# Retention attention with a SoLU layer behind it: two neighbouring tokens on a partition, fewer and longer loads, some transposes by DMA, and w_out centred once

## The chip, the cores and the metric

The kernel runs on one core of a Trainium2 chip. The core has the engines PE (matmul, with its weight loads), DVE (VectorE), ACT (ScalarE), POOL (GpSimd) and SP, which here only hands out DMA transfers, and sixteen DMA engines. The time is the device time of one execution in microseconds (us), as the median of several runs.

## What is computed

A retention attention without softmax over 8 batches, 8 heads, 576 tokens and a head size of 64, then a layer with SoLU, layer norm and an output projection over the 4608 tokens. Inputs and output are float32.

```python
scores = (q @ k.T) / sqrt(64)
rel = pos[:, None] - pos[None, :]
ret = scores * where(rel >= 0, gamma[h] ** rel, 0)      # gamma[h] = 1 - 2 ** (-5 - h)
x = (ret @ v)                                            # [4608, 512] after joining the heads
h = x @ w_in                                             # [4608, 1024]
e = exp(h - max(h)); solu = h * e / (sum(e) + 1e-9)
ln = (solu - mean(solu)) / sqrt(var(solu) + 1e-6) * g_ln
out = ln @ w_out                                         # [4608, 512]
```

## The kernel before

**Tiles.** Two batches are worked on side by side, one on partitions 0 to 63 and one on 64 to 127. A *pair* is 128 tokens of each of the two batches; 576 tokens make four long pairs and a short one of 64 tokens, and 4 times 2 batches make 20 pairs, four of them short. Each pair gives *chunks* of 128 tokens for the layer behind the attention: two from a long pair, one from a short one, 36 in all, numbered 0 to 35.

**Loads.** `load` (line 165) brings q, k and v of a pair as float32 into a ring of 14 slots in SBUF, one slot a tensor and pair. Each tensor of a long pair takes four transfers: two groups of 64 tokens (`s`) for each of two batches (`x`). A partition holds the tokens p and p + 64, and each piece that is contiguous in DRAM is one head's 64 numbers, 256 bytes.

**Attention.** `cast` (line 191, and 117 or 115 where no table is applied) makes float16 copies, with powers of gamma multiplied into q and v. `turn` (line 215) transposes q and k on PE against an identity, eight 128 x 128 blocks a tensor, into PSUM; `back` copies them to SBUF (`qT`, `kT`). `sc` (line 279) multiplies; a long pair's scores are three blocks of 64 tokens for each head, since the fourth is in the future. `mask` (line 303, steps `m0` and `m1`) multiplies with the 0/1 table `keep`. `kp`, `t`, `s16` and `s32` carry the state on from pair to pair, `xs` applies it, `xv` (line 391) adds the values, `xT` copies a chunk's x, already transposed, to SBUF.

**The layer.** `mm1` (line 483) gives h in two PSUM banks; `max` (line 501), `exp` (526), `solu` (558, with the sum of its result), `nmu` (565), `uc` (572: subtracts the mean), `sq` (579: sum of squares), `w1`, `w2` (586) and `pow` (592) give the factor of the layer norm. `lp` (601) transposes the centred tile on PE, `uT` copies it out, `mm2` (623) multiplies with `w_out16`, which has g_ln in it, and `osb` (643 on ACT, 639 on DVE) scales the rows into one of four output tiles. `st` (line 657; 654 for pair 0 and the short pairs) sends the tile to DRAM.

**Order.** Nothing is scheduled while it runs. The string `PLAN` lists every step with its tile, its engine (`@v` DVE, `@s` ACT, `@g` POOL) and its PSUM banks, and each engine works through its own part in that order. All loads and stores stand in SP's queue, in the plan's order: a transfer that has to wait holds back all that stand behind it. At the start, `warm` puts matmuls on zeros between the first steps.

Of the kernel before, what the change touches and what calls it, by code (L numbers as in the profile page):

```python
# [17 lines left out]
def _np_tables():  # L18


    g = 1.0 - 2.0 ** (-5.0 - np.arange(H, dtype=np.float64))
    i = 64 * np.arange(2)[None, :] + (np.arange(P) % 64)[:, None]
    gq = (g[None, None, :] ** i[:, :, None]) / 8.0
    gk = g[None, None, :] ** (-i[:, :, None])
    gs = np.zeros((P, 4))
    for e in range(2):
        for hp in range(4):
            gs[e * 64 : e * 64 + 64, hp] = g[2 * hp + e] ** 128.0
    return np.concatenate([gq.reshape(P, 16), gk.reshape(P, 16), gs], axis=1).astype(np.float32)
# [3 lines left out]
def kernel(  # L33
# [19 lines left out]
    CROSS = 2  # L53
    SPLIT = (35,)
# [25 lines left out]
    small = sb.tile([P, 36], FP, name="small")  # L80
    gq = small[:, 0:16].rearrange("p (s h) -> p s h", s=2)
    gk = small[:, 16:32].rearrange("p (s h) -> p s h", s=2)
    gs = small[:, 32:36]
    keep = sb.tile([P, 192], FP, name="keep")
    ident = sb.tile([P, P], F16, name="ident")
    zeros = sb.tile([P, 512], F16, name="zeros")
    mhalf = sb.tile([P, 1], FP, name="mhalf")
# [3 lines left out]
    w_x16 = sb.tile([P, 4, DFF], F16, name="w_x16") if CROSS else None  # L91
    w_out16 = sb.tile([P, NF, DM], F16, name="w_out16")
    ring = sb.tile([P, 14, 1024], FP, name="ring")
# [10 lines left out]
    def banks(bs):  # L104
        if len(bs) == 1:
            return pb[:, bs[0] : bs[0] + 1]
        a, b = bs[:2]
        return pb[:, a : b + 1 : b - a]
# [31 lines left out]
    def halves(n, j):  # L140
        if j is not None:
            return [j]
        return [0] if short(n) else [0, 1]

    def span(n, j):
        hs = halves(n, j)
        return slice(hs[0], hs[-1] + 1)


    def slot(name, n):  # L150
        i = "qkv".index(name)
        if n < 2:
            return (0, 7)[n] + i
        return (3 * (n - 2) + i) % 14

    def tok(name, n):
        return ring[:, slot(name, n)].rearrange("p (s h d) -> p s h d", s=2, h=H)

    def load(name, src, n, j):
        g, c = pairs[n]  # L160
        t = tok(name, n)
        for s in halves(n, j):
            for x in range(2):
                r = 64 * (2 * c + s)
                nc.sync.dma_start(  # L165
                    out=t[64 * x : 64 * x + 64, s],
                    in_=src[2 * g + x, :, r : r + 64, :].rearrange("h p d -> p h d"),
                )
# [16 lines left out]
    def cast(name, n, j, eng, table):  # L185
        for s in halves(n, j) if table is not None else [span(n, j)]:
            src, t = tok(name, n)[:, s], t16(name, n)[:, s]
            if table is None:
                copy(eng, t, src)
            else:  # L190
                vec(eng).tensor_tensor(  # L191
                    out=t, in0=src, in1=table[:, s].unsqueeze(2).to_broadcast([P, H, D]),
                    op=ALU.mult,
                )
# [14 lines left out]
    def turn(name, n, j, bs):  # L209
        t = pb[:, bs[0]].bitcast(F16).rearrange("p (s a c) -> p s a c", s=2, a=4)  # L210
        src = t16(name, n)
        for s in halves(n, j):
            s2 = src[:, s].rearrange("p h d -> p (h d)")
            for hp in range(4):
                nc.tensor.transpose(
                    out=t[:, s, hp], in_=s2[:, hp * P : (hp + 1) * P], identity=ident
                )
# [5 lines left out]
    def back(name, n, j, eng):  # L223
        b = T["t" + name, n, j]
        hs = span(n, j)
        w = slice(hs.start * 256, hs.stop * 256)
        t = turned(name, n).rearrange("p s a c -> p (s a c)")
        if eng == "s":
            copy("s", words(t)[:, w], pb[:, b, w])
        else:  # L230
            w2 = slice(w.start * 2, w.stop * 2)
            copy("v", t[:, w2], pb[:, b].bitcast(F16)[:, w2])
# [19 lines left out]

    def blocks(n, j):
        if short(n) or j == 0:
            return 0, 1
        return (1, 3) if j == 1 else (0, 3)

    def per_bank(n, j):
        lo, hi = blocks(n, j)
        return 8 // (hi - lo) if hi - lo < 3 else 2  # L260

    def scores(n, j, bs, e, hp):
        lo, hi = blocks(n, j)
        w = 64 * (hi - lo)
        k = min(per_bank(n, j), 4)
        at = w * (hp % k)
        return pb[:, bs[2 * (hp // k) + e], at : at + w]

    @step
    def sc(n, j, eng, bs):  # L270
        lo, hi = blocks(n, j)
        qt, kt = turned("q", n), turned("k", n)

        def one(e, hp, key, a, b):
            r = slice(64 * e, 64 * e + 64)
            o = scores(n, j, bs, e, hp)[:, 64 * (a - lo) : 64 * (b - lo)]
            for x in range(2):
                c = slice(64 * x, 64 * x + 64)
                nc.tensor.matmul(  # L279
                    out=o[c], lhsT=kt[r, key, hp, c],  # L280
                    rhs=qt[r, a - key : b - key, hp, c], start=True, stop=True,
                )

        rows = []
        for e in range(2):
            rows.append([])
            for hp in range(4):
                a, b = max(lo, 0), min(hi, 2)
                rows[e].append((b - a, lambda e=e, hp=hp, a=a, b=b: one(e, hp, 0, a, b)))
                if hi == 3:  # L290
                    rows[e].append((1, lambda e=e, hp=hp: one(e, hp, 1, 2, 3)))
        together(rows)
        T["sc", n, j] = bs

    def ret(n):
        return buf("ret", n, 2, [P, 2, 4, 192], F16)

    def mask(n, j, i):
        lo, hi = blocks(n, j)
        k = min(per_bank(n, j), 4)  # L300
        bs = T["sc", n, j][2 * i : 2 * i + 2]
        w = 64 * (hi - lo)
        nc.vector.tensor_tensor(  # L303
            out=ret(n)[:, :, k * i : k * i + k, 64 * lo : 64 * hi],
            in0=banks(bs)[:, :, 0 : k * w].rearrange("p e (a c) -> p e a c", a=k),
            in1=keep[:, 64 * lo : 64 * hi].unsqueeze(1).unsqueeze(1).to_broadcast([P, 2, k, w]),
            op=ALU.mult,
        )
# [14 lines left out]
    def xs(n, j, eng, bs):  # L323
        T["x", n, j] = bs
        qt = turned("q", n)
        hs = span(n, j)
        a, b = hs.start * 64, hs.stop * 64
        st = T["s16", n]
        w = b - a

        def one(x, e, hp):
# [3 lines left out]
                out=o[out_half(n, x, e), hp, a:b], lhsT=st[r, x, hp],  # L335
                rhs=qt[r, hs, hp, 64 * x : 64 * x + 64],
# [3 lines left out]
        rows = [[], []]  # L340
        if crossed(n):
            for hp in range(4):
                for e in range(2):
                    rows[e].append((w, lambda e=e, hp=hp: (one(0, e, hp), one(1, e, hp))))
        else:
            for x in range(2):
                for hp in range(4):
                    for e in range(2):
                        rows[e].append((w, lambda x=x, e=e, hp=hp: one(x, e, hp)))
        together(rows)  # L350
# [9 lines left out]
    def kp(n, j, eng, bs):  # L360
        k16, v16 = t16("k", n), t16("v", n)

        def one(x, s, hp):
            r = slice(64 * x, 64 * x + 64)
            o = pb[:, bs[x], 0:256].rearrange("p (a d) -> p a d", a=4)
# [8 lines left out]
            [(64, lambda x=x, s=s, hp=hp: one(x, s, hp)) for hp in range(4) for s in range(2)]  # L374
            for x in range(2)
        ])
        T["kp", n] = bs

    @step
    def xv(n, j, eng, bs):  # L380
        old = ("x", n, j) in T
        bs = T.setdefault(("x", n, j), bs)
        lo, hi = blocks(n, j)
        v16 = t16("v", n)
        rt = ret(n)

        def one(x, key, hp, a, b):
            r = slice(64 * x, 64 * x + 64)
            o = pb[:, bs[x]].rearrange("p (a c) -> p a c", a=4)
            for e in range(2):  # L390
                nc.tensor.matmul(  # L391
                    out=o[out_half(n, x, e), hp, 64 * (a - key) : 64 * (b - key)],
                    lhsT=v16[r, key, 2 * hp + e], rhs=rt[r, e, hp, 64 * a : 64 * b],
                    start=not old and key == 0 and hp == 0, stop=True, skip_group_check=True,
                )

        rows = []
        for x in range(2):
            rows.append([])
            for hp in range(4):  # L400
                a, b = lo, min(hi, 2)
                rows[x].append((b - a, lambda x=x, hp=hp, a=a, b=b: one(x, 0, hp, a, b)))
                if hi == 3:
                    rows[x].append((1, lambda x=x, hp=hp: one(x, 1, hp, 2, 3)))
        together(rows)
# [5 lines left out]
    def t(n, j, eng, bs):  # L411
        g, c = pairs[n]
        kp = banks(T["kp", n])[:, :, 0:256].rearrange("p x (a d) -> p x a d", a=4)
        s = state("ts", n, FP)
        if c == 0:
# [26 lines left out]
    def xT(m, j, eng, bs):  # L442
        n, i = pair_of[m]
        eng = eng or "s"
        if short(n) or n == 0:
            src = banks(T["x", n, i if n == 0 else None]).rearrange("p x (a c) -> p x a c", a=4)
            copy(
                eng, xt(m).rearrange("p a (x c) -> p x a c", x=2),
                src[:, :, :, 64 * i : 64 * i + 64],
            )  # L450
        else:
            b = T["x", n, None][i]
# [43 lines left out]
    def tiny(name, m, j=None, depth=6):  # L496
        return buf(name + sfx(j), m, depth, [P, 1], FP)
# [17 lines left out]
    def u_of(m):  # L515
        return buf("u", m, 2, [P, DFF], F16)

    def uc_of(m):
        return buf("uc", m, 3, [P, DFF], F16)
# [29 lines left out]
    @step  # L549
    def w1(m, j, eng, bs):  # L550
        s = tiny("s", m)
        nc.gpsimd.tensor_scalar(
            out=tiny("w1", m), in0=s, scalar1=s, scalar2=1e-6 * DFF, op0=ALU.mult, op1=ALU.mult
        )
# [23 lines left out]
    def sq(m, j, eng, bs):  # L578
        nc.scalar.activation(  # L579
# [283 lines left out]
```

## Time and profile before

| | |
|---|---|
| Median of three runs | 250.69 us (249.96 to 250.76) |
| The profiled execution | 250.73 us |
| Its span, from the first instruction to the last | 249.0 us |
| Mean granted clock of PE | 0.978 |
| DMA in all | 43.53 MB in 122532 packets, 116096 of them under 512 bytes |
| Landing of a load of 128 KB, median | 3.4 to 3.5 us |

The profile gives for each engine the time in which it was busy, in groups of equal instructions; the waits, with the engine that ended them; stretches of the span with the busy time of each engine; and the chain that ended last, which is followed back from the last instruction to whatever released it at each step. "SPq" is SP's queue at work on handing out transfers, and a line number is that of the kernel. The time from issue to landing of a transfer is taken up to its completion.

### The profile page before, as it was taken

What the parts mean: (1) busy time and instruction counts of PE and PEld (TensorE: products, weight loads), DVE (VectorE), ACT (ScalarE), POOL (GpSimd) and SP (SyncE); (2) the same over time, 40 slices, a digit from 0 to 9 for tenths busy, and PEclk for the clock granted to TensorE, in tenths of its full rate; (3) what the DMA queues carried; (4) which work ended last, traced back from release to release, by engine and by line L of the source; (5) the groups of instructions that cost most, each with busy time, mean ns of one, the idle gap of its engine ahead of it and who ended that gap; (6) DMA issues with size and microseconds to landing.
All of it is one profiled execution on the core that took longest, in us unless ns stands there. A gap on an engine that the chain in (4) does not pass through costs nothing.

```text
span 249.0 us, 7816 instructions
## 1 busy us (share of the span) xinstructions
PE 215.7 (87%) x3175; PEld 120.8 (49%) x3175; DVE 196.3 (79%) x342; ACT 152.9 (61%) x278; POOL 146.0 (59%) x196
## 2 busy tenths in 40 slices
PE   8997878967988887987569999899959999999992
PEld 2543534542553554544326754565527455555642
DVE  0646869993989977688708999997968999999971
ACT  1334747562873677638706858788747667577881
POOL 2054459672777785498356279469398917653330
PEclk9999999997999999999958999999999999999999
DMA  5997898797788788787888887887766446411025
GB/s 114 217 323 165 187 282 191 172 227 158 180 181 244 170 185 201 160 219 209 181 188 203 202 212 196 192 228 205 176 149 202 99 143 155 129 46 42 3 87 170
DMA packets 122532, 43.53 MB, mean 175 GB/s; under 512 B 116096, under 2 KB 116352, under 8 KB 122368
## 3 DMA queue, kind: packets, MB, share of 16 engines
q1 hardware_dynamic: 122352, 43.01, 70.0%
q8 instruction: 25, 0.41, 0.7%
q14 instruction: 11, 0.09, 0.1%
q10 hardware_dynamic: 144, 0.02, 0.1%
HBM read 32.53 MB, written 9.44 MB: 169 GB/s over the span
## 4 chain that ended last, share of the span: by engine, by line
SPq 28%; PE 26%; DVE 16%; DMA 15%; issue 5%; POOL 5%; ACT 3%; DVEq 0%; ACTq 0%; POOLq 0%
SPq L165 23%; PE pb L623 10%; PE pb L483 7%; DMA ring<-in_q_dram 5%; DMA ring<-in_v_dram 4%; DVE u L558 4%; DVE nm L501 3%; DMA ring<-in_k_dram 3%; DMA ring<-in_moe_w_out_dram 3%; DVE ret L303 3%; PE pb L601 3%; POOL v L191 2%; DVE uc L572 2%; SPq L654 2%; PE pb L391 1%
## 5 line engine op out<-in xcount | busy, mean ns | idle before, releaser
L623 PE MATMUL pb<-w_out,uT 128*128 128x512 f16 (+1 forms) x296 | 67.0, 374 | 5.6 <-DVE uT L117 2.5
L526 ACT ACTIVATE e<-pb,nm 128x1024 f32<-128x1024 f32 (+1 forms) x37 | 40.4, 1092 | 17.9 <-DVE nm L501 15.0
L501 DVE TENSOR_REDUCE nm<-pb 128x1 f32<-128x1024 f32 x35 | 42.3, 1217 | 10.2 <-PE pb L483 10.0
L191 POOL TENSOR_TENSOR v<-ring,small 128x512 f16<-128x512 f32 x35 | 36.9, 1072 | 15.1 <-DMA ring<-in_v_dram 15.1
L483 PEld LDWEIGHTS <-xT 128*128 128x128 f16 x280 | 27.0, 100 | 36.6 <-issue 9.1
L623 PEld LDWEIGHTS <-uT 128*128 128x128 f16 x296 | 27.7, 98 | 34.5 <-issue 6.6
L558 DVE SCALAR_TENSOR_TENSOR u<-pb,e 128x1024 f16<-128x1024 f32 (+1 forms) x37 | 43.9, 1187 | 0.6 <-ACT e L526 0.2
L579 ACT ACTIVATE sq<-uc 128x1024 f16<-128x1024 f16 (+1 forms) x37 | 38.4, 1039 | 9.0 <-DVE uc L572 7.1
L483 PE MATMUL pb<-w_in,xT 128*128 128x512 f16 x168 | 39.9, 379 | 1.9 <-DVE w_in L117 1.7
L191 POOL TENSOR_TENSOR q<-ring,small 128x512 f16<-128x512 f32 x30 | 31.5, 1060 | 14.8 <-DMA ring<-in_q_dram 12.3
L303 DVE TENSOR_TENSOR ret<-pb,keep 128x768 f16<-128x768 f32 (+2 forms) x36 | 32.0, 917 | 0.5 <-PE pb L279 0.5
L483 PE MATMUL pb<-w_x,xT 128*128 128x512 f16 x112 | 29.5, 411 | 2.6 <-DMA w_x<-w_in 2.6
L592 POOL TENSOR_TENSOR rs<-w,mhalf 128x1 f32<-128x1 f32 x36 | 20.0, 561 | 19.7 <-DVE w L586 16.0
L572 DVE TENSOR_SCALAR uc<-u,nmu 128x1024 f16<-128x1024 f16 (+1 forms) x37 | 26.5, 719 | 1.0
L643 ACT ACTIVATE osb<-pb,rs 128x512 f32<-128x512 f32 x26 | 17.5, 686 | 15.3 <-POOL rs L592 6.3
L115 ACT CAST xT<-pb 128x512 f16<-128x512 f32 x28 | 15.7, 588 | 13.8 <-PE pb L391 13.8
L601 PE MATMUL pb<-ident,uc 128*128 128x128 f16 x288 | 21.6, 220 | 2.9 <-DVE uc L572 2.9
L115 ACT COPY uT<-pb 128x512 f32<-128x512 f32 x30 | 17.2, 586 | 9.5 <-PE pb L601 9.4
L117 POOL CAST k<-ring 128x1024 f16<-128x1024 f32 (+1 forms) x14 | 13.2, 945 | 16.3 <-DMA ring<-in_k_dram 16.3
L423 POOL TENSOR_TENSOR s<-ts,small 128x512 f16<-128x512 f32 x16 | 17.4, 1089 | 7.2 <-DVE ts L418 5.1
L601 PEld LDWEIGHTS <-uc 128*128 128x128 f16 x288 | 17.1, 98 | 8.9 <-DVE uc L572 5.7
L716 PE MATMUL pb<-zeros 128*128 128x512 f16 x63 | 18.6, 425 | 1.2 <-DVE mhalf L818 1.2
(62 smaller groups left out, 255.5 us busy)
## 6 DMA issues: line engine op xcount, KB each, us to landing
ring<-in_k_dram SPq DMA_DIRECT2D x72, 128.0 KB, 3.4
ring<-in_q_dram SPq DMA_DIRECT2D x72, 128.0 KB, 3.5
ring<-in_v_dram SPq DMA_DIRECT2D x72, 128.0 KB, 3.4
out_dram<-osb SPq DMA_DIRECT2D x30, 256.0 KB, 3.0
ring<-in_moe_w_in_dram SPq DMA_DIRECT2D x4, 512.0 KB, 5.4
ring<-in_moe_w_out_dram SPq DMA_DIRECT2D x4, 512.0 KB, 8.8
out_dram<-osb SPq DMA_DIRECT2D x10, 128.0 KB, 2.8
w_x<-w_in SPq DMA_DIRECT2D x2, 512.0 KB, 4.8
```

Of the source, the lines that this page charges most:

```text
L115: nc.scalar.copy(out=out, in_=in_)
L165: nc.sync.dma_start(out=t[64 * x : 64 * x + 64, s], in_=src[2 * g + x, :, r : r + 64, :].rearrange("h p d -> p h d"),)
L191: vec(eng).tensor_tensor(out=t, in0=src, in1=table[:, s].unsqueeze(2).to_broadcast([P, H, D]), op=ALU.mult,)
L303: nc.vector.tensor_tensor(out=ret(n)[:, :, k * i : k * i + k, 64 * lo : 64 * hi], in0=banks(bs)[:, :, 0 : k * w].rearrange("p e (a c) -> p ...
L483: nc.tensor.matmul(out=pb[:, bs[i]], lhsT=s[:, d], rhs=w[:, d, i * 512 : (i + 1) * 512], start=r == 1, stop=r == 4,)
L501: nc.vector.tensor_reduce(out=tiny("nm", m, j), in_=h_of(m, j), axis=AX.X if j is not None else AX.XY, op=ALU.max, negate=True,)
L526: nc.scalar.activation(out=like_h(e_of(m), j), in_=h_of(m, j), func=ACT.Exp, bias=tiny("nm", m), accum_out=tiny("s", m, j),)
L558: nc.vector.scalar_tensor_tensor(out=like_h(u_of(m), j), in0=h_of(m, j), scalar=1.0, in1=like_h(e_of(m), j), op0=ALU.mult, op1=ALU.mult, a ...
L572: nc.vector.tensor_scalar(out=uc_of(m)[:, cols(j)], in0=u_of(m)[:, cols(j)], scalar1=tiny("nmu", m), scalar2=None, op0=ALU.add, op1=ALU.by ...
L579: nc.scalar.activation(out=buf("sq", 0, 1, [P, DFF], F16)[:, cols(j)], in_=uc_of(m)[:, cols(j)], func=ACT.Square, accum_out=tiny("ss", m, j),)
L601: nc.tensor.transpose(out=t[:, c], in_=u[:, a * P : (a + 1) * P], identity=ident)
L623: nc.tensor.matmul(out=pb[:, bs[0], 0:w], lhsT=ut(m)[:, c], rhs=w_out16[:, c, a : a + w], start=c == 0, stop=c == NF - 1,)
```

## The change

**Two neighbouring tokens on a partition.** Partition p of a long pair now holds the tokens 2p and 2p + 1 instead of p and p + 64, so that each contiguous piece of a load is 128 numbers, and one transfer a tensor and batch is enough: six a pair instead of twelve. The tables of powers follow the new places of the tokens.

```diff
-    i = 64 * np.arange(2)[None, :] + (np.arange(P) % 64)[:, None]
+    p = np.arange(P) % 64
+    i = np.stack([2 * p, 2 * p + 1, p], axis=1)
...
-        for s in halves(n, j):
-            for x in range(2):
-                r = 64 * (2 * c + s)
-                nc.sync.dma_start(
-                    out=t[64 * x : 64 * x + 64, s],
-                    in_=src[2 * g + x, :, r : r + 64, :].rearrange("h p d -> p h d"),
-                )
+        for x in both(j):
+            t = ring[64 * x : 64 * x + 64, slot(name, n)]
...
+                t = t.rearrange("p (h d) -> p h d", h=H)
+                s = src[2 * g + x, :, P * c : P * c + P, :].rearrange("h (p s) d -> p h (s d)", s=2)
+            nc.sync.dma_start(out=t, in_=s)
```

The scores of a long pair are now four blocks of 64 tokens for each head instead of three, because either place of a partition can be before the other one's token; `mask` works on 1024 instead of 768 columns, and `keep` is [128, 5, 64]. The output of a chunk of a long pair has the rows in the order of the places, and the store puts them back in order:

```diff
             r = (2 * g + i) * S + c * P
-            q_.dma_start(out=out[r : r + P, a : a + w], in_=t)
+            q_.dma_start(
+                out=out[r : r + P, a : a + w].rearrange("(p s) m -> s p m", s=2), in_=t
+            )
```

Chunks of pair 0 are stored in this way too; only the short pairs keep the two stores of 64 rows.

**q and k of six pairs transposed by DMA.** For the pairs 7, 8, 10, 12, 13 and 15 the steps `dq` and `dk` take the place of `tq`, `qT`, `tk` and `kT`:

```diff
+    def by_dma(name, n):
+
+        k = 4 * len(places(n))
+        nc.sync.dma_start_transpose(
+            out=turned(name, n).rearrange("p s a c -> p (s a) c")[:, 0:k],
+            in_=t16(name, n).rearrange("p s h d -> p (s h d)")[:, 0 : k * P],
+        )
```

**w_out centred from chunk 8 on.** With `RAW = 8`, chunks from 8 on leave `uc` out: `lp` transposes the tile as it is, `sq` takes the mean as the bias of its square, and `mm2` multiplies with `w_mid16`, a second copy of w_out from which the mean of each column is taken away. The copy is made once, in eight steps `ce` on DVE; `mean` and `evm` give the column means by eight matmuls and a copy.

```diff
     def uc_of(m):
-        return buf("uc", m, 3, [P, DFF], F16)
+        return buf("uc", m, 3, [P, DFF], F16) if m < RAW else u_of(m)
...
     def sq(m, j, eng, bs):
+        by = {} if m < RAW else {"bias": tiny("nmu", m)}
...
+    def ce(c, j, eng, bs):
+        nc.vector.scalar_tensor_tensor(
+            out=w_mid16[:, c], in0=w_out32[:, c], scalar=g32[:, c : c + 1], in1=mean_sb,
+            op0=ALU.mult, op1=ALU.subtract,
+        )
```

w_out in float32 now has a place of its own, and the ring of loads has 10 slots instead of 14. `w1`, `w2` and `pow` are done once for the two chunks of a pair, on [128, 2], but for the first pair and pair 18.

**First pair by halves.** The first pair is loaded, cast, turned, scored and masked by batch, 64 partitions at a time, instead of by groups of 64 tokens; its first `mm1` begins after the first batch. Where before had 63 warming matmuls, there are now 31.

**The plan.** The whole string `PLAN` is written anew, with the new steps in it.

More of the change, by code (lines that the diff above doesn't have):

```diff
@@ L138, in step, with places, rows, both @@
         return f
-    def halves(n, j):
-        if j is not None:
-            return [j]
+    def places(n):
         return [0] if short(n) else [0, 1]
-    def span(n, j):
-        hs = halves(n, j)
-        return slice(hs[0], hs[-1] + 1)
+    def rows(j):
+        return slice(0, P) if j is None else slice(64 * j, 64 * j + 64)
+    def both(j):
+        return [0, 1] if j is None else [j]
     def slot(name, n):
@@ L185, in cast @@
     def cast(name, n, j, eng, table):
[L186 to L194, printed above, removed]
+        r = rows(j)
+        ns = len(places(n))
+        src = ring[r, slot(name, n), 0 : ns * 512].rearrange("p (h s d) -> p s h d", s=ns, h=H)
+        t = t16(name, n)[r, 0:ns]
+        if table is None:
+            copy(eng, t, src)
+            return
+        for s in range(ns):
+            by = table[r, 2 if short(n) else s].unsqueeze(2).to_broadcast([t.shape[0], H, D])
+            vec(eng).tensor_tensor(out=t[:, s], in0=src[:, s], in1=by, op=ALU.mult)
     @step
@@ L248, in kT, with scores @@
         back("k", n, j, eng or "s")
[L253 to L267, printed above, removed]
+    def scores(n, bs, e, hp, s):
+        if short(n):
+            return pb[:, bs[e], 64 * hp : 64 * hp + 64]
+        at = (2 * (hp % 2) + s) * P
+        return pb[:, bs[2 * (hp // 2) + e], at : at + P]
@@ L284, in sc @@
[L284 to L292, printed above, removed]
+                    out=scores(n, bs, e, hp, s)[c], lhsT=kt[r, s, hp, c],
+                    rhs=qt[r, 0:ns, hp, c], start=True, stop=True,
+                )
@@ L293, in sc, with kept @@
+        together([
+            [(1, lambda e=e, hp=hp, s=s: one(e, hp, s)) for hp in range(4) for s in places(n)]
+            for e in range(2)
+        ])
         T["sc", n, j] = bs
     def ret(n):
-        return buf("ret", n, 2, [P, 2, 4, 192], F16)
+        return buf("ret", n, 2, [P, 2, 2, 2, 2 * P], F16)
+    def kept(n, x, e, hp, s):
+        r = slice(64 * x, 64 * x + 64)
+        if short(n):
+            return ret(n)[r, 0, e].rearrange("p a c -> p (a c)")[:, 64 * hp : 64 * hp + 64]
+        return ret(n)[r, hp // 2, e, hp % 2, P * s : P * s + P]
@@ L298, in mask @@
     def mask(n, j, i):
-        lo, hi = blocks(n, j)
-        k = min(per_bank(n, j), 4)
+        r = rows(j)
+        p = r.stop - r.start
         bs = T["sc", n, j][2 * i : 2 * i + 2]
[L302 to L308, printed above, removed]
+        out = ret(n)[r, i].rearrange("p e a c -> p e (a c)")
@@ L373, in kp @@
         together([
[L374 to L375 removed]
+            [(1, lambda x=x, s=s, hp=hp: one(x, s, hp)) for hp in range(4) for s in range(2)]
+            for x in both(j)
         ])
[L377 removed]
+        T["kp", n, j] = bs
     @step
@@ L382, in xv, with one @@
         bs = T.setdefault(("x", n, j), bs)
-        lo, hi = blocks(n, j)
         v16 = t16("v", n)
-        rt = ret(n)
-        def one(x, key, hp, a, b):
+        w = 64 * len(places(n))
+        def one(x, s, hp):
             r = slice(64 * x, 64 * x + 64)
-            o = pb[:, bs[x]].rearrange("p (a c) -> p a c", a=4)
+            o = pb[:, bs[x if j is None else 0]].rearrange("p (a c) -> p a c", a=4)
             for e in range(2):
                 nc.tensor.matmul(
-                    out=o[out_half(n, x, e), hp, 64 * (a - key) : 64 * (b - key)],
-                    lhsT=v16[r, key, 2 * hp + e], rhs=rt[r, e, hp, 64 * a : 64 * b],
-                    start=not old and key == 0 and hp == 0, stop=True, skip_group_check=True,
-                )
[L397 to L405, printed above, removed]
+                    out=o[out_half(n, x, e), hp, 0:w], lhsT=v16[r, s, 2 * hp + e],
+                    rhs=kept(n, x, e, hp, s), start=not old and s == 0 and hp == 0, stop=True,
+                    skip_group_check=True,
+                )
+        together([
+            [(1, lambda x=x, s=s, hp=hp: one(x, s, hp)) for hp in range(4) for s in places(n)]
+            for x in both(j)
+        ])
     def state(name, n, dtype):
```

358 lines of the change are left out of this document (193 added, 165 removed).

## The prediction

> **What bounds the kernel now.** I read the page's shares first, then the chain that ended last, then stretches of time.
>
> ```profile
> span 249.0 us, 7816 instructions
> PE 215.7 (87%) x3175; PEld 120.8 (49%) x3175; DVE 196.3 (79%) x342; ACT 152.9 (61%) x278; POOL 146.0 (59%) x196
> ...
> SPq 28%; PE 26%; DVE 16%; DMA 15%; issue 5%; POOL 5%; ACT 3%; DVEq 0%; ACTq 0%; POOLq 0%
> SPq L165 23%; PE pb L623 10%; PE pb L483 7%; DMA ring<-in_q_dram 5%; DMA ring<-in_v_dram 4%; DVE u L558 4%; DVE nm L501 3%; DMA ring<-in_k_dram 3%; DMA ring<-in_moe_w_out_dram 3%; DVE ret L303 3%; PE pb L601 3%; POOL v L191 2%; DVE uc L572 2%; SPq L654 2%; PE pb L391 1%
> ```
>
> PE is busiest, but the longest entry of the chain is SP's queue handing out the loads of line 165: 23% of 249.0 us, 57 us. The view of that line shows why:
>
> ```profile
> L165 SPq DMA_DIRECT2D ring<-in_k_dram x72: 595/633/3674, 0.8 to 193.6; - x72
> L165 SPq DMA_DIRECT2D ring<-in_q_dram x72: 595/634/2518, 2.3 to 208.8; - x72
> L165 SPq DMA_DIRECT2D ring<-in_v_dram x72: 595/633/1872, 6.3 to 203.8; - x72
> ```
>
> Each of 216 loads holds SP for 0.633 us (median), 137 us together, up to 208.8 us. The stretches (columns: stretch, its length, busy time of PE, weight load, DVE, ACT, POOL, granted clock, DMA share, GB/s) show what the compute engines reach meanwhile:
>
> ```profile
> 65.00:205.00 140.00, 122.60 (x1924) 70.83 (x1925) 117.79 (x204) 92.01 (x167) 93.89 (x119) 0.98 0.76 188
> 144.00:165.00 21.00, 20.14 (x337) 11.58 (x336) 19.94 (x37) 15.55 (x30) 15.86 (x21) 1.00 0.82 199
> ```
>
> Where nothing is late PE is busy 20.14 of 21 us (96%); over the whole middle 122.6 of 140 (88%). So before, the middle is a mixture: PE and DVE near their limit, with late loads in between.
>
> **The stores, which decide.** The 30 whole stores of before are 128 rows of 2 KB:
>
> ```profile
> L657 SPq DMA_DIRECT2D out_dram<-osb x30: 332/432/2144, 76.1 to 243.9; - x30
> DMA to landing us min/median/max: 2.1/3.0/4.5
> ```
>
> After, a partition holds token 2p or 2p+1, so the rows of one 128-partition tile go to DRAM in the order "all even tokens, then all odd ones". In the changed program's list of SP's instructions these 32 stores (256 KB each) have a destination of 2 x 64 rows of 512 numbers, against 128 partitions on the SBUF side. Everything that before moves begins with a count of 64 or 128 on both sides. The trace shows no transfer that begins with 2, so its cost has two ends. If it is still shared by 16 DMA engines, it stays at 3.0 us to landing. If a transfer is shared out by whole steps of its first count, the two sides have only 2 such steps in common, and two engines carry 64 rows (128 KB) each. [...]
>
> [...]
>
> What can an engine carry? Four stretches say it:
>
> ```profile
> 16.00:24.00 8.00, 6.31 (x31) 2.71 (x29) 3.69 (x5) 3.07 (x6) 4.04 (x4) 1.00 0.91 191
> 220.00:244.00 24.00, 23.67 (x250) 13.21 (x235) 20.93 (x50) 19.12 (x39) 8.68 (x17) 1.00 0.15 56
> 13.00:16.00 3.00, 3.00 (x75) 1.58 (x74) 1.31 (x3) 1.24 (x2) 1.14 (x3) 1.00 1.01 385
> 32.00:34.00 2.00, 2.00 (x11) 0.88 (x9) 0.01 (x1) 0.07 (x1) 1.26 (x2) 1.00 1.08 389
> ```
>
> The last two are backlogs, and the share stops at about 1: an engine takes one packet after another, so times add. 16 to 24 us holds loads alone, in rows of 256 bytes: 191/0.91/16 = 13.1 GB/s an engine, 19.5 ns a row. 220 to 244 us holds stores alone: 56/0.15/16 = 23.3 GB/s, 88 ns a row of 2 KB. (The best of any stretch is 385/1.01/16 = 23.8.) The new loads have rows of 512 bytes, which before has not; on the straight line through the two that is 29 ns, 17.5 GB/s. Its ends are 13.1 and 23.3.
>
> **The sum, for one of the two engines.**
> - Stores: 32 x 131,072 bytes at 23.3 GB/s = 5.63 us each, 180 us (176 at 23.8).
> - Loads of the 16 long pairs: 96 of 256 KB, a sixteenth each, 16,384 bytes at 17.5 = 0.94 us: 90 us (68 to 120 at the ends).
> - Loads of the four short pairs: 24 x 8,192 bytes at 13.1: 15 us.
> - Weights and the crossed copy: 10 x 32,768 bytes at 23.3: 14 us.
> - DMA transposes, which before has not: 12 of 256 KB, 16,384 bytes an engine, at 23.3 or, as rows of 256 bytes, at 13.1: 0.70 to 1.25 us each. Between ends so near I take 1.0: 12 us.
> - Short stores, ten, still by 64 rows: 3 us.
>
> Together 314 us for engines that can start at 1 us. That is more than the 249.0 of the whole span, so the two engines set the end; the rest is how well they are kept fed. Before the first such store SP's list has 30 long and 6 short loads and the ten transfers of weights, 28 + 4 + 14 = 46 us of it. In the trace the first store stands at
>
> ```profile
> 65.74 1.22 SPq L654 DMA_DIRECT2D out_dram<-osb  x2
> ```
>
> behind an SP queue full of loads; with 120 loads instead of 216 it comes earlier. I put it at 50 us, so 4 us idle. The other 314 - 46 = 268 us follow, and 2 us for the last landing (2.1 was the least): span 320, and 1.7 more for the execution around it (250.73 against 249.0). An engine that is fed can be a little better than these averages, so I round down to **320 us**. The profiled execution of before (250.73) lies at the upper end of its runs (median 250.69), so no correction is needed.
>
> Does the wait reach the compute engines? The output tile has four buffers, and already before
>
> ```profile
> SPq L657 <- ACT osb L643: 24.6, 6, 8.6
> ACT osb L643 <- DMA out_dram<-osb: 5.8, 2, 3.1
> ```
>
> SP stands 24.6 us before stores whose tile isn't written, and ACT 5.8 us before tiles whose store isn't out. After, the second grows: a chunk costs an engine 5.6 us for its store and 2.8 us for half a pair's loads, 8.4, against (249 - 65.7)/36 = 5.1 us at which before finishes chunks from its first store on. Four tiles on, ACT's scaling of the output (or DVE's) waits for a landing; behind it stand exp, the squares and the PSUM copies, so DVE and PE wait next, and the load queue behind the next store on SP.
>
> **The other edits cost nothing here, because the two engines' 314 us cover them.** What they would be without that cover:
>
> ```profile
> L572 DVE TENSOR_SCALAR uc<-u,nmu 128x1024 f16<-128x1024 f16 x35 | 25.9, 740 | 0.9
> L558 DVE SCALAR_TENSOR_TENSOR u<-pb,e 128x512 f16<-128x512 f32 x2 | 1.4, 691 | 0.2 <-ACT e L526 0.2
> L303 DVE TENSOR_TENSOR ret<-pb,keep 128x768 f16<-128x768 f32 x30 | 27.4, 946 | 0.2 <-PE pb L279 0.2
> L303 DVE TENSOR_TENSOR ret<-pb,keep 128x1024 f16<-128x1024 f32 x1 | 1.2, 1224 | 0.3 <-PE pb L279 0.3
> L586 DVE TENSOR_TENSOR w<-w,ss 128x1 f32<-128x1 f32 x36 | 12.2, 344 | 3.6 <-POOL w L552 3.3 <-ACT sq L579 0.3
> L215 PE MATMUL pb<-ident,q 128*128 128x128 f16 x144 | 12.1, 222 | 1.2 <-POOL q L191 0.7 <-DVE q L191 0.5
> L215 PE MATMUL pb<-ident,k 128*128 128x128 f16 x144 | 11.8, 225 | 1.0 <-POOL k L117 0.9
> ```
>
> DVE: 27 centrings gone (-20.0), eight centrings of w_out, priced as the half-width product (+5.5), 30 masks of 1024 instead of 768 (+8.3), 14 of 36 sums gone (-4.8): -11 us. PE: q and k of six pairs are 96 transposes at 23.9/288 = 83 ns (-8.0), while scores and values with 128 columns throughout add about 2.7: -5 us in the middle; 8 matmuls for the column means and 32 fewer warming ones lie near the start. SP: 216 loads become 120 (137 to 76 us), and the 12 transposes stand in the same queue, each behind POOL's cast of q or k, with all later loads and stores queued behind it. First pair by halves: six issues of 0.633 us instead of twelve, up to 4 us earlier. The ring of 10 slots for 14 costs nothing where the engine, not the slot, is late.
>
> **Rivals.**
> - *The stores keep 16 engines: faster.* Then each is 8 rows an engine, 0.70 us, the DMA sum falls to 314 - 180 + 22 = 156 us, and SP no longer sets the pace. Four engines are enough for this: 134 + 90 = 224 us, below the span of before. The middle goes to PE's 96%: (122.6 - 5.3)/0.96 = 122 instead of 140, and 250.7 - 18 = **233 us**. For it: nothing in the trace forbids it. Against it: the first counts 2 and 128. 10 in 100.
> [...]
> - *Two engines, and badly fed: slower still.* SP stops at a store whose tile isn't written, the loads behind it don't leave, and the two engines run dry. If each of 32 stores leaves a gap as long as an empty landing less its transfer (2.1 - 0.7 = 1.4 us), 45 us: **365**. Against it: several transfers are in flight at once. 5 in 100.
>
> **How the numbers follow.** Two engines and fed 83 in 100; the rivals 10, 2 and 5. For the likeliest I take 300 (5.5 us a store by 23.8 GB/s, 0.78 a load by 21 GB/s, and no idle time: 295 + 5) to 345 (25 us of gaps); this holds 80 in 100 over all cases, so it is the range. About 0.3% is what the measurement can tell from no change: faster 0.10, same 0.02, slower 0.88.
>
> **What will show it.** Right: the landing of a whole store 7 us or more instead of 3.0; ACT and DVE waiting tens of us for the output's DMA; a mean DMA share near (2 x 314 + 14 x 134)/16/320 = 0.5 instead of the 0.76 of the middle, because 14 engines idle; PE's share near 65%. Issues of 120 loads near 0.6 us each show SP relieved without profit. Wrong: stores landing in 3 us, or a span under 249. If they land late and the span is still under 300, the price of a row was too high.

## The result, and the profile after

The changed kernel takes 352.0 us (median of four runs, 351.78 to 356.77) against 250.32 us before (249.83 to 250.76): a ratio of 1.4108 [1.3984, 1.4232]. That is 32 us above the forecast and 7 us above the upper end of its range.

The page of the changed kernel, rows that answer to those shown of before:

```profile
span 350.1 us, 7355 instructions
PE 230.3 (66%) x3039; PEld 127.8 (37%) x3039; DVE 188.9 (54%) x311; ACT 154.8 (44%) x276; POOL 138.7 (40%) x171
...
DMA  8999999873897359599133959989475221210121
...
DMA packets 84033, 46.64 MB, mean 133 GB/s; under 512 B 28448, under 2 KB 77856, under 8 KB 83872
...
q1 hardware_dynamic: 83856, 46.15, 69.0%
...
DMA 41%; SPq 16%; PE 15%; POOL 8%; issue 7%; DVE 4%; ACT 4%; ACTq 0%; POOLq 0%; DVEq 0%
```

DVE and POOL have less work than before (188.9 against 196.3 us, 138.7 against 146.0); every engine has a smaller share of the span. The chain has moved: before, SP's queue had 28% of it and transfers 15%; now transfers have 41%, and the 16% of SP are what is left of its queue. Some of its last steps (start, duration, what) show what such a transfer is:

```profile
257.07 6.63 DMA ring<-in_k_dram
...
269.83 13.26 DMA out_dram<-osb
...
285.10 7.99 DMA out_dram<-osb
...
293.78 1.23 ACT sq L591 x2
...
296.17 5.71 SPq L171
...
301.93 8.98 DMA ring<-in_v_dram
...
313.01 1.73 PE pb L639 x8
...
317.36 1.35 PE pb L639 x7
...
319.27 1.26 ACT osb L659 x2
...
320.64 12.39 DMA out_dram<-osb
```

A whole store stands in the chain for 12 to 13 us, where before its median from issue to landing was 3.0; the store of 7.99 us is a half one of a short pair, handed out by line 670. Who waits for it is in the view of waits (us in total, times, longest):

```profile
ACT osb L659 <- DMA out_dram<-osb: 75.8, 10, 22.4
POOL q L198 <- DMA ring<-in_q_dram: 50.4, 5, 24.6
PEld L290 <- DMA kT<-k: 34.1, 3, 21.9
...
POOL v L198 <- DMA ring<-in_v_dram: 27.0, 9, 8.6
```

ACT's wait for the output's DMA went from 5.8 us to 75.8. SP's queue has fewer entries, but slower ones (least/median/most in ns, first to last in us):

```profile
L171 SPq DMA_DIRECT2D ring<-in_q_dram x40: 601/891/4436, 0.8 to 253.8; - x40
L171 SPq DMA_DIRECT2D ring<-in_k_dram x40: 595/1075/3271, 1.6 to 286.4; - x40
L171 SPq DMA_DIRECT2D ring<-in_v_dram x40: 600/910/5707, 3.6 to 301.9; - x40
L673 SPq DMA_DIRECT2D out_dram<-osb x32: 511/594/4732, 59.3 to 335.2; - x32
L244 SPq DMA_TRANSPOSE qT<-q x6: 1279/2989/6211, 93.3 to 223.0; - x6
L244 SPq DMA_TRANSPOSE kT<-k x6: 1266/3457/9965, 97.0 to 233.0; - x6
```

A load's issue is still 0.6 us at best, but 0.89 to 1.08 at the median, and a DMA transpose holds SP for 3.0 to 3.5 us at the median. Over time (columns as in the prediction):

```profile
36.00:47.00 11.00, 10.57 (x154) 5.77 (x156) 9.33 (x16) 6.81 (x14) 8.92 (x10) 0.89 1.18 201
50.00:100.00 50.00, 35.73 (x506) 20.61 (x505) 33.74 (x51) 26.27 (x48) 27.98 (x31) 0.90 0.80 169
150.00:200.00 50.00, 25.68 (x398) 14.70 (x399) 21.92 (x34) 16.87 (x30) 16.54 (x21) 0.73 0.69 113
```

From 36 to 47 us, before the first whole store at 59.3 us, the DMA engines carry 201 GB/s and PE is busy 10.57 of 11 us. From 150 to 200 us the rate is 113 GB/s and PE is busy half of the time.

### The profile page after: what moved, and what is told of

Read it like the earlier page. It is cut to its first block, busy times and chain, and to the rows that moved or that the text cites. A ratio compares the mean times of both kernels' runs of the same rounds, so it can differ in the third digit from the quotient of the medians.

```text
span 350.1 us, 7355 instructions
## 1 busy us (share of the span) xinstructions
PE 230.3 (66%) x3039; PEld 127.8 (37%) x3039; DVE 188.9 (54%) x311; ACT 154.8 (44%) x276; POOL 138.7 (40%) x171
## 2 busy tenths in 40 slices
DMA packets 84033, 46.64 MB, mean 133 GB/s; under 512 B 28448, under 2 KB 77856, under 8 KB 83872
## 4 chain that ended last, share of the span: by engine, by line
DMA 41%; SPq 16%; PE 15%; POOL 8%; issue 7%; DVE 4%; ACT 4%; ACTq 0%; POOLq 0%; DVEq 0%
DMA out_dram<-osb 18%; SPq L171 12%; DMA ring<-in_v_dram 8%; DMA ring<-in_k_dram 6%; PE pb L491 5%; DMA ring<-in_q_dram 5%; PE pb L639 4%; DMA kT<-k 3%; POOL v L198 2%; SPq L673 2%; POOL q L198 2%; PE pb L617 2%; DVE ret L325 1%; POOL s L434 1%; ACT e L539 1%
## 5 line engine op out<-in xcount | busy, mean ns | idle before, releaser
L639 PE MATMUL pb<-w_mid,uT 128*128 128x512 f16 (+1 forms) x232 | 59.0, 408 | 14.1 <-ACT osb L659 14.1
L659 ACT ACTIVATE osb<-pb,rs 128x512 f32<-128x512 f32 (+1 forms) x32 | 21.3, 682 | 95.5 <-DMA out_dram<-osb 75.8
L325 DVE TENSOR_TENSOR ret<-pb,keep 128x1024 f16<-128x1024 f32 (+2 forms) x38 | 42.9, 1161 | 33.6 <-PE pb L290 33.4
L198 POOL TENSOR_TENSOR q<-ring,small 128x512 f16<-128x512 f32 x33 | 34.7, 1073 | 51.7 <-DMA ring<-in_q_dram 50.4
L198 POOL TENSOR_TENSOR v<-ring,small 128x512 f16<-128x512 f32 (+1 forms) x37 | 38.7, 1065 | 30.3 <-DMA ring<-in_v_dram 27.0
L290 PE MATMUL pb<-qT,kT 64*64 64x128 f16 (+1 forms) x576 | 14.7, 242 | 33.4 <-DMA kT<-k 26.9
L591 ACT ACTIVATE sq<-u,nmu 128x1024 f16<-128x1024 f16 (+1 forms) x29 | 32.5, 1123 | 0.8 <-DVE nmu L576 0.5
L606 POOL TENSOR_TENSOR rs<-w,mhalf 128x2 f32<-128x2 f32 (+1 forms) x22 | 15.0, 682 | 33.7 <-DVE w L598 24.7
L405 PE MATMUL pb<-ret,v 64*64 64x128 f16 (+1 forms) x576 | 14.3, 235 | 17.6 <-ACT osb L659 8.0
L290 PEld LDWEIGHTS <-kT 64*64 64x64 f16 x576 | 11.3, 124 | 38.9 <-DMA kT<-k 34.1
L617 PE MATMUL pb<-ident,u 128*128 128x128 f16 x224 | 19.1, 234 | 4.8 <-ACT osb L659 4.7
L443 POOL TENSOR_TENSOR s<-ts,small 128x512 f32<-128x512 f32 x12 | 13.1, 1091 | 19.1 <-DVE ts L427 18.1
```

The costliest lines, as they stand in the source:

```text
L198: vec(eng).tensor_tensor(out=t[:, s], in0=src[:, s], in1=by, op=ALU.mult)
L290: nc.tensor.matmul(out=scores(n, bs, e, hp, s)[c], lhsT=kt[r, s, hp, c], rhs=qt[r, 0:ns, hp, c], start=True, stop=True,)
L325: nc.vector.tensor_tensor(out=out, in0=src, in1=by, op=ALU.mult)
L591: nc.scalar.activation(out=buf("sq", 0, 1, [P, DFF], F16)[:, cols(j)], in_=uc_of(m)[:, cols(j)], func=ACT.Square, accum_out=tiny("ss", m, ...
L617: nc.tensor.transpose(out=t[:, c], in_=u[:, a * P : (a + 1) * P], identity=ident)
L639: nc.tensor.matmul(out=pb[:, bs[0], 0:w], lhsT=ut(m)[:, c], rhs=(w_out16 if m < RAW else w_mid16)[:, c, a : a + w], start=c == 0, stop=c = ...
```

## The experiments

Each ratio is to the kernel before measured beside the run, whose median lay between 248.15 and 249.58 us. Theory: the 32 whole stores run on two engines. Its rival: another part of the change (the transposes in SP's queue, or the loads) costs the time.

### Each store as two transfers

```diff
-            q_.dma_start(
-                out=out[r : r + P, a : a + w].rearrange("(p s) m -> s p m", s=2), in_=t
-            )
+            for s in range(2):
+                q_.dma_start(
+                    out=out[r : r + P, a : a + w].rearrange("(p s) m -> s p m", s=2)[s],
+                    in_=t[64 * s : 64 * s + 64],
+                )
```

> The changed kernel with each of the 32 whole stores sent as two transfers, one for each place of a partition, so that each begins with 64 on both sides; all else as in the change. Theory A (a store that begins with 2 runs on two DMA engines, and these set the end): 230 to 255 us, and ACT hardly waits for stores. Theory B (the DMA transposes hold SP's queue and the engines, the stores are a sideshow): over 300 us. Theory C (half of each): about 290 us.

Measured: 255.59 us (254.95 to 256.44), ratio 1.0318 [1.0222, 1.0415]. Same rows to the same places, 96 us less. The page of this kernel:

```profile
span 253.4 us, 7406 instructions
...
DMA packets 84993, 46.64 MB, mean 184 GB/s; under 512 B 29408, under 2 KB 78816, under 8 KB 84832
...
q1 hardware_dynamic: 84816, 46.16, 91.3%
...
out_dram<-osb SPq DMA_DIRECT2D x70, 128.0 KB, 3.3
```

ACT's wait for the output is nearly gone:

```profile
ACT osb L659 <- DMA out_dram<-osb: 8.6, 3, 7.5
```

The small packets count the engines. Bytes and rows are those of the changed kernel, yet there are 29408 packets under 512 bytes instead of 28448, 960 more. If each engine that takes part in a transfer adds one small packet at its end, 64 transfers on 16 engines in place of 32 on 2 give 64 x 16 - 32 x 2 = 960. The trace has a second sign. It records when each packet starts and how long it takes, so one can count how many are in flight at once: exactly two are for 93.2 us of the changed kernel, and for 2.1 us of this one.

### The same store in the kernel before, alone

```diff
-            q_.dma_start(out=out[r : r + P, a : a + w], in_=t)
+            q_.dma_start(
+                out=out[r : r + P, a : a + w].rearrange("(p s) m -> s p m", s=2), in_=t
+            )
```

> The kernel before with one edit: its 30 whole stores begin with 2 (the rows of a tile go out in the order of the change, so they land in other rows than the reference's). Same bytes, same issues. Theory A: the two engines carry 30 x 5.63 = 169 us of stores, 216 x 0.625 = 135 us of loads, 14 us of weights and 4 us of short stores, 322 us, and the time is 322 to 345 us. Theory B: under 265 us, as SP and the loads are those of before.

Measured: 343.82 us (342.6 to 345.21), ratio 1.387 [1.376, 1.3979]. One rearranged address pattern on 30 stores, the same bytes, and the kernel before is as slow as the changed one. First the packets of before, then this kernel's page and its first wait:

```profile
DMA packets 122532, 43.53 MB, mean 175 GB/s; under 512 B 116096, under 2 KB 116352, under 8 KB 122368
```

```profile
span 340.9 us, 7816 instructions
...
DMA packets 122111, 43.51 MB, mean 128 GB/s; under 512 B 115676, under 2 KB 115932, under 8 KB 121948
```

```profile
ACT osb L643 <- DMA out_dram<-osb: 58.6, 8, 15.5
```

The small packets fall by 420 = 30 x (16 - 2), and ACT's wait for the output grows from 5.8 us to 58.6. Neither long loads nor transposes are needed for it.

### Four engines

```diff
-                    out=out[r : r + P, a : a + w].rearrange("(p s) m -> s p m", s=2)[s],
-                    in_=t[64 * s : 64 * s + 64],
+                    out=o.rearrange("(p a) m -> a p m", a=4), in_=t[64 * s : 64 * s + 64]
```

Here `o` is the destination of the line above.

> The changed kernel with each whole store sent by place as in the run with mended stores, but with a destination that begins with 4 (4 x 16 rows; the rows of a tile go to other places than the reference's). The forecast said that four engines are enough: 134 + 90 = 224 us of transfers, so the time would be that of the mended stores, 255 us. If the loads and the transposes cost the engines what the share of 91.3% in the run with mended stores says (0.913 x 253 = 231 us, of which 40 are stores), the four engines carry 191 + 90 = 281 us, and the time is 280 to 300 us.

Measured: 293.22 us (291.83 to 295.13), ratio 1.1856 [1.175, 1.1962]. The page and the first wait:

```profile
DMA packets 84225, 46.64 MB, mean 161 GB/s; under 512 B 28640, under 2 KB 78048, under 8 KB 84064
```

```profile
ACT osb L659 <- DMA out_dram<-osb: 39.0, 8, 13.8
```

192 small packets more than in the changed kernel are 64 x 4 - 32 x 2, so each half ran on four engines; exactly four packets are in flight for 33.5 us, in the changed kernel for 6.6. Two, four and sixteen engines give 352, 293 and 256 us, and ACT waits 75.8, 39.0 and 8.6 us for the output. The time goes with the number of engines, as the theory says, but four are not enough to hide the stores.

### Without the DMA transposes

Here `dq` and `dk` of six pairs became `tq`, `qT`, `tk` and `kT` again; the first of the twelve places:

```diff
-        k:7@g dq:7 exp:9 solu:9 mm1:10/23 kT:6@s pow:3 max:10 mm2:6/7 osb:6@s v:7@g sc:6/4501 m1:6
+        k:7@g tq:7/5 qT:7@s exp:9 solu:9 mm1:10/23 kT:6@s pow:3 max:10 mm2:6/7 osb:6@s v:7@g sc:6/4501 m1:6
```

> The changed kernel with q and k of the six pairs transposed on PE again and copied out by ACT (a free PSUM bank at the place in the plan where the transpose by DMA stood); the stores as in the change. Theory A: the two engines lose only the transposes' share, 12 us by the forecast and at most 60, so 295 to 345 us. Theory B: under 265 us. Theory C: about 300 us.

> Both edits together: stores by place, and the six pairs' transposes on PE. Theory A: within 10 us of the kernel with only the stores mended, 230 to 255 us. Theory B: 230 to 255 us too, but then far below the kernel with only the stores mended. If the transposes by DMA are a gain by themselves, this is slower than the stores mended alone.

Measured: 343.06 us (341.06 to 344.52), ratio 1.3832 [1.3707, 1.3957], with the stores on two engines; 263.16 us (262.62 to 263.45), ratio 1.0612 [1.0534, 1.069], with the halved stores. So the transposes cost 7 to 9 us where two engines are late (weight loads of PE wait 34.1 us for `kT` there, and 6.5 us with the halved stores), and save 7.6 us where they are not. They are no rival for the whole loss of about 100 us.

### Loads to 128 partitions

The changed loads bring 512-byte pieces to 64 partitions. Here, from the second long pair on, a transfer brings pieces of the same length, as many bytes and as many transfers, to 128 partitions:

```diff
+        if n and not short(n):
+            r = min(P * c, S - 2 * P)
+            for x in range(2):
+                t = ring[:, slot(name, n), 512 * x : 512 * x + 512]
+                s = src[2 * g, 4 * x : 4 * x + 4, r : r + 2 * P, :]
+                nc.sync.dma_start(
+                    out=t.rearrange("p (h d) -> p h d", h=4),
+                    in_=s.rearrange("h (p s) d -> p h (s d)", s=2),
+                )
+            return
```

> The run with mended stores, and from the second pair on each load of a long pair covers 128 partitions and 4 heads instead of 64 partitions and 8 heads: the same number of transfers, bytes and pieces of 512 bytes, but tokens of one batch alone, so the output is not the reference's. [...] Theory L (a piece of 512 bytes costs what it costs, 42 ns): share and time stay, 253 to 258 us.

> The changed kernel with its stores on two engines, and with the loads over 128 partitions of the run 'wide' (tokens of one batch alone, so the output is not the reference's). The step in question is the price of a piece of 512 bytes, 0.94 us a load in the forecast: in a backlog the loads of the change ran at 201 GB/s, 1.30 us a load, 35 us more over 96 loads. If this price is what made 352 of 320, then loads at about 300 GB/s (0.87 us) give 315 to 325 us. If the gap comes from elsewhere (engines run dry between stores, SP held by the transposes), it stays above 340 us.

Measured: with halved stores 235.15 us (234.46 to 235.66), ratio 0.9497 [0.941, 0.9584]; with the stores of the change 330.73 us (328.77 to 334.17), ratio 1.3195 [1.3102, 1.3288]. The 64 partitions cost 20 us in the one and 21 us in the other. To compare rates, a stretch must be a backlog and hold these loads alone; in the two below, by the packet records, 98% of the bytes or more are in pieces of 512 bytes. First the kernel with halved stores and loads to 64 partitions, then the one with halved stores and loads to 128:

```profile
36.00:40.00 4.00, 4.00 (x18) 1.69 (x17) 2.91 (x8) 1.39 (x4) 2.89 (x4) 0.89 1.24 212
```

```profile
30.00:34.00 4.00, 2.99 (x74) 2.39 (x75) 3.96 (x8) 1.38 (x4) 3.04 (x4) 0.50 1.21 295
```

The 256-byte pieces of before, in backlog, stand in a stretch of the kernel that has the loads of before and its stores on two engines, ahead of its first whole store:

```profile
36.00:47.00 11.00, 8.69 (x164) 4.98 (x163) 9.88 (x18) 7.28 (x14) 9.46 (x12) 1.00 1.02 191
```

So pieces of 512 bytes to 64 partitions move 212 GB/s and pieces of 256 bytes 191; pieces of 512 bytes to 128 partitions move 295. A load of 256 KB takes 1.24 us in the one and 0.89 us in the other. In a full backlog that is 31 us for 90 such loads; not all of them stand in one, and 20 to 21 us are measured. (The 201 GB/s of the changed kernel from 36 to 47 us hold a quarter of 256-byte pieces, the loads of a short pair.) The edit changes more than the width: it reads the rows of one batch twice over instead of those of two batches, and four heads a transfer instead of eight. No run separates this from the width.

To the kernel with wide loads and its stores on two engines the transposes on PE were added:

> The run 'wide_two' (stores on two engines, loads over 128 partitions, output not the reference's) with the six pairs' transposes on PE. Of the 32 us by which the forecast fell short, the loads' price was 21 (352 to 330.7). If the rest is the transposes by DMA, which the forecast had at 1.0 us of an engine each and which held SP for 1.3 to 10 us each: 316 to 324 us, the forecast's 320 less its 12 us for them, and what feeding costs. If the rest is engines that run dry behind SP's order: 327 to 333 us.

Measured: 328.38 us (323.94 to 330.78), ratio 1.3037 [1.2875, 1.32]. The interval overlaps that of the kernel with them (1.3195), so the times tell nothing of the transposes here. ACT still waits 45.2 us for the output.

### Whole stores in the tile's own order

Rows go to DRAM as they lie in the tile, so one store of 128 rows per tile, as before:

```diff
-            q_.dma_start(
-                out=out[r : r + P, a : a + w].rearrange("(p s) m -> s p m", s=2), in_=t
-            )
+            q_.dma_start(out=out[r : r + P, a : a + w], in_=t)
```

> The changed kernel with each whole store as one transfer of 128 rows in the tile's own order, as before had it (the rows of a long pair's chunk land in the order of the places, so the output is not the reference's). Against the run with mended stores (255.6 us), which sends two of 64 partitions: if the halves cost something by themselves (32 more issues of 0.6 us on SP, 64 partitions a transfer), 250 to 253 us; if the loads and transposes alone make the mended kernel slower than before, 254 to 257 us.

Measured: 250.0 us (248.12 to 252.4, ten runs), ratio 1.005 [1.0004, 1.0096].

```profile
span 248.9 us, 7355 instructions
...
DMA packets 84481, 46.64 MB, mean 187 GB/s; under 512 B 28896, under 2 KB 78304, under 8 KB 84320
```

28896 - 28448 = 448 = 32 x (16 - 2), the count of engines once more. 102 us, the whole loss, lie in the order of the stored rows. What is left of the change is worth nothing: its ratio is 1.005. The halved stores (255.59) cost 5.6 us more than these.

### Why the mended kernel isn't faster than before

Four runs looked for what keeps the kernel with halved stores above before.

Half of the loads issued by ACT, to free SP:

```diff
-            nc.sync.dma_start(out=t, in_=s)
+            (nc.scalar if x == 1 and n > 1 else nc.sync).dma_start(out=t, in_=s)
```

> The run with mended stores, and from the third pair on the loads of the second batch (partitions 64 to 127) are issued by ACT instead of SP. [...] If ACT's queue stands before full slots, it is slower, up to 275 us. Theory L: no faster than 205 GB/s.

Measured: 317.82 us (311.82 to 319.95), ratio 1.2689 [1.248, 1.2898], far above the 275 us that were expected at most. The waits:

```profile
POOL q L198 <- DMA ring<-in_q_dram: 36.9, 7, 8.6
...
ACT osb L659 <- POOL rs L606: 30.4, 9, 6.0
...
DVE u L569 <- ACT e L539: 26.0, 15, 6.5
```

A load in ACT's order leaves only when ACT comes to it, and POOL waits 36.9 us for q instead of the 17.1 of the kernel with halved stores:

```profile
POOL q L198 <- DMA ring<-in_q_dram: 17.1, 5, 8.3
```

The run doesn't tell whether SP's issues are the bound of the mended kernel.

Only the centring of w_out, put into the kernel before (`RAW = 8`, w_out in float32 in a tile of its own, a third buffer for `u`); one of its edits:

```diff
-        return buf("uc", m, 3, [P, DFF], F16)
+        return buf("uc", m, 3, [P, DFF], F16) if m < RAW else u_of(m)
```

> The kernel before with one part of the change alone: w_out centred from chunk 8 on (27 whole and 2 half centrings on DVE go, 20.7 us; eight steps for the centred copy come, 5.5 us; 8 matmuls and a copy for the means). Loads, stores and transposes as before. If DVE's work is on the path in the middle, 240 to 247 us; if loads and PE hide it, 248 to 252 us.

Measured: 250.43 us (248.13 to 251.18), ratio 1.0106 [1.001, 1.0202]: no gain, though 27 whole centrings of 0.74 us and two half ones leave DVE and eight of w_out take their place.

The ring of loads with 14 slots again:

```diff
-    ring = sb.tile([P, 10, 1024], FP, name="ring")
+    ring = sb.tile([P, 14, 1024], FP, name="ring")
...
-        return (3 * (n - 2) + i) % 10
+        return (3 * (n - 2) + i) % 14
```

> The run with mended stores (255.6 us), with 14 slots in the ring of loads as before instead of 10. If the loads come late for want of slots: 245 to 252 us. If the DMA engines, 91% busy, set the pace: 253 to 258 us.

Measured: 256.01 us (254.21 to 258.56), ratio 1.0181 [1.0094, 1.0268]. The interval overlaps that with 10 slots (1.0318), so the two are not told apart.

17 more warming matmuls, at four places:

```diff
-        mm1:0.0/23 v:0.1@g warm:1/0 kp:0.1/0 cw:1.1@s m0:0.1 m1:0.1 xv:0.1/4 cw:1.0@g t:0.1 wi:2
+        mm1:0.0/23 v:0.1@g warm:5/0 kp:0.1/0 cw:1.1@s m0:0.1 m1:0.1 xv:0.1/4 cw:1.0@g t:0.1 wi:2
```

> The run with mended stores, with 17 more warming matmuls at four places of the start where one warming step stands already (31 become 48; before had 63). The granted clock of the mended kernel is 0.5 from 14 to 19 us and from 28 to 36 us, where before has 1.0; w_x and w_in matmuls of these stretches take twice as long. If this delays what follows: 3 to 7 us faster, 249 to 253 us, and the clock near 1 up to 36 us. If the late loads set the pace after it anyway: 254 to 257 us.

Measured: 258.73 us (254.19 to 262.17), with too much spread for a ratio. First a stretch of the kernel with halved stores, then the same stretch of this kernel:

```profile
28.00:32.00 4.00, 2.03 (x81) 1.69 (x77) 2.65 (x5) 1.36 (x3) 3.92 (x6) 0.50 1.05 315
```

```profile
28.00:32.00 4.00, 2.83 (x65) 1.89 (x64) 1.04 (x1) 2.90 (x5) 3.92 (x6) 1.00 1.08 310
```

The granted clock there rose from 0.50 to 1.00, and no gain can be seen in the time.

So besides the halved stores (5.6 us) only the loads to 64 partitions are shown to cost, 20 us. But the loads of before go to 64 partitions too, so their width alone doesn't explain why the mended kernel is above before; what uses up the work that the change saves stays open. The kernel with wide loads is the only one below before; a layout in which such loads bring the tokens that the attention needs was not tried, and none of the kernels with the reference's tokens and rows beat the kernel before.

## Why the prediction was right, and where it was wrong

**Two engines: right, and shown.** The packets count them, the store alone slows the kernel before by 95 us, and without it the changed kernel is at 250.0. That a store is shared out by whole steps of its first count was an assumption of the author; the counts of small packets give 2 engines for a first count of 2, 4 for 4, and 16 for 64 and 128.

**Where the wait goes: right.** ACT waits 75.8 us for the output's landing, POOL then for the loads behind the stores on SP (50.4 us for q, 27.0 for v); PE's share is 66% (forecast 65%).

**The price of a load: the step that failed.** The prediction took 0.94 us for a load of 256 KB, 90 us in its sum for 96, from the straight line between rows of 256 bytes and of 2 KB. In backlog these loads run at 212 GB/s, 1.24 us each and 13.2 GB/s an engine, at the low end of its own range. The line's lower point came from loads to 64 partitions and its upper one from stores of 128, so it mixed the length of a piece with the number of partitions: in the run with wide loads the same pieces take 0.89 us a load, close to the 0.94. Nor was the lower point clean: by the packet records a fifth of the bytes from 16 to 24 us are weights in packets of 4 KB, not loads in rows of 256 bytes.

**What the miss is made of.** The packet records show it. They don't name the engine, so a time with any packet in flight is the most that either late engine can have worked, and a time with none is the least that it stood idle; each column is one execution, in us.

| | Forecast | Changed kernel | Its loads to 128 partitions | Its transposes on PE |
|---|---|---|---|---|
| Some packet in flight | 314 | 334.4 | 310.5 | 321.1 |
| None, between the first and the last | 4 | 12.0 | 14.8 | 17.9 |
| Ahead of the first and behind the last | 2 | 3.6 | 3.6 | 3.6 |
| Span | 320 | 350.1 | 328.9 | 342.7 |

Of the 30 us by which the span is longer, at most 20 are transfers and at least 8 gaps. With wide loads the transfers come to 310.5, so the sum of 314 holds but for the loads to 64 partitions. They cost 24 us here, less than the 31 of a full backlog: where at most two packets are in flight, a piece of 512 bytes takes 32 ns on average in the changed kernel, against 45 with more than 16.

**Feeding.** The first whole store stood at 59.3 us and not at 50, but nothing was lost by it: up to 150 us some packet is always in flight. The gaps come later; the longest, 5.4 us from 315.7 on, ends with whole stores for whose tiles the chain shows PE and ACT at work until just before 320.64. That 120 load issues would stay near 0.6 us was a wrong sign to look for; their median is 0.89 to 1.08.

**The range.** It gave the loads an upper end of 120 us, 30 more than it used, but its upper bound of 345 was built from gaps alone. With that end in the sum the time is 314 + 30 + 4 + 2 + 1.7 = 352. That it meets the measured time is in part luck, since at least 8 us of the miss are gaps; but the text had the price and didn't carry it into the bound.

**Transposes.** 12 us in the sum; by the table 13 us of transfers go with them, of which 6 come back as gaps, and the kernel is 7 to 9 us faster. The size was fair. But their packets are recorded for far longer: 0.690 x 350.1 = 241.6 us of engine time with them, 0.539 x 342.7 = 184.7 without, 57 us where the sum had 12, of which some 7 are load packets that got shorter too. This and the price of loads are why the DMA share was 0.69 and not the forecast 0.5.

**The rivals.** Their sizes can be read from the kernels that do use 16 engines, though the changed one doesn't. "Four engines are enough, 224 us" falls: four engines took 293. The 233 us falls too, since the mended kernel is at 255.59: its loads are hardly cheaper by the byte than those of before (212 against 191 GB/s), and no run shows a gain from the relief of SP. With whole stores it is at 250.0, and with halved ones the transposes save 7.6 us. "Badly fed", 365, had 45 us of gaps, where the records show 12.

## What to carry to other kernels

When a store reorders rows, look at the outermost count of its DRAM side: a leading 2 put 256 KB on two engines and cost 95 to 102 us here, and two plain transfers undid nearly all of it. Price loads by what the stretch in backlog moved, not by the piece length: loads to 64 partitions ran at 191 GB/s with pieces of 256 bytes and at 212 with 512, loads to 128 partitions at 295. See that such a stretch holds one kind of transfer alone. A bound that was worked out for one term must be in the range, even when the text prefers a value near the middle.

## What was not expected of the hardware

- The share of the DMA engines passes 1 (1.18 in the changed kernel, 1.24 with halved stores), where the prediction had it stop at about 1: times of packets overlap, so GB/s is the measure of a backlog, and 1 minus the share isn't idle time.
- A DMA transpose of 256 KB holds SP for 1.2 us at least, which before could not show, and up to 9.97 us with the two engines late. With halved stores the medians are 1.35 and 1.42 us:

```profile
L244 SPq DMA_TRANSPOSE qT<-q x6: 1289/1348/2794, 82.6 to 171.6; - x6
L244 SPq DMA_TRANSPOSE kT<-k x6: 1233/1418/1807, 86.1 to 180.7; - x6
```

- The granted clock was lower in the changed kernel: 0.73 from 150 to 200 us, where PE is busy 25.68 of 50 us, against 0.98 before from 65 to 205 us, where it is busy 122.60 of 140. PE's busy time grew from 215.7 to 230.3 us for 136 matmuls fewer than before.
